# Nyström attention and sticky experts on one core: the preload of w1 behind batch 1's first sums, with other filling products, transfers and score halves in the start-up

## The chip, the core and the metric

The kernel runs on one core of one Trainium2 chip. The metric is the device time of one execution in microseconds; 451.7 us is the median of 3 runs of the kernel before (451.6 to 452.22). The engines are named as in the profile: PE (TensorE matmul), PEld (its weight loads), DVE (VectorE), ACT (ScalarE), POOL (GpSimd), SP (SyncE, which issues nearly all transfers).

## What is computed

For each of 8 batches a Nyström attention with 8 heads, 576 tokens and 32 landmarks is computed, and its output goes through one of 8 experts per token; the expert of a token may stick to that of the token before it.

```python
def sm(a, b):
    s = scale * np.matmul(a, b.transpose(0, 1, 3, 2)); s = s - np.max(s, axis=-1, keepdims=True)
    e = np.exp(s); return e / (np.sum(e, axis=-1, keepdims=True) + 1e-09)
A, Bm, C = sm(q, k_lm), sm(q_lm, k_lm), sm(q_lm, k)      # q_lm, k_lm: means over 18 tokens, 32 of them
Z = Bm.T / (norm1(Bm) * norminf(Bm) + 1e-06)
for _ in range(6):
    Z = 2 * Z - Z @ Bm @ Z
x = A @ Z @ C @ v                                        # (8 batches, 576 tokens, 512)
logits = x @ w_gate; local = sigmoid(x @ w_local)
# per token: e = argmax(logits) if local < 0.5 or first token, else the expert of the token before
out = softmax(logits)[e] * (relu(x @ w1[e]) @ w2[e])     # w1[e]: 512 x 1024, w2[e]: 1024 x 512
```

## The kernel before

Work is done batch by batch. For each batch one "own" expert, the one that most of its tokens chose, is applied to all 576 tokens; tokens of other experts are gathered later into extra slots. x is never formed: w1 is first multiplied by the small matrix `wt` (`w_w1`, L1247, 16 matmul records; PSUM result split into a high part `gh` on ACT and a low part `gl` on DVE, `split_g`), and then `mm1` (L1295) multiplies that with the attention weights `at` (high and low part, `ath` and `atl`). Per block f of 128 hidden units `mm1` has six products, in the order gh ath, gh atl, gl ath for each half g of the heads; their relu goes through ACT and DVE, and the products with w2 follow (L1337). The eight blocks f are made in two passes over the tokens.

The order on each engine is written out by hand: every engine runs its instructions in program order, `at_time` hangs steps into a clock that `expert` advances, and `startup` is a plain list. `startup` does batch 0's attention and parts of batch 1's. Its order around the change:

- Before anything else PE multiplies zeros with zeros (L190: 11 products of 512 columns, L192: 18 of 16 columns), into a tile that nobody reads. PE's next step is `score_c(0, 0)` (L965).
- SP issues all loads of batches 0 and 1, and then (L945) `firsts`: of every one of the 8 experts the first 128 hidden units of w1, 2 MB, so that they are there when the expert becomes known. After that SP issues nothing until the write of `wt` (L751) and that of the attention weights (L1165).
- POOL computes half sums of batch 1's landmarks (`lk0_half`, L310) between two steps of batch 0's softmax (`sa_max`, L1070).
- When the vote on the gates has written the expert's number into `regs` (L875), PE fills the time with 3 `keep_busy` products and 22 narrow ones (L1175); SP and PE load the number into a register; SP issues the expert's w1 and w2 (`load_w1`, L1232, f = 1, 2, 3 and two pairs, and `get_w2`, L1274); PE multiplies the preloaded piece (`first_w1`, L1257), which gives block f = 0.
- `second_block` (at clock 0.02) begins with batch 1's scores of landmarks against all keys (`c_products`, L621): 512 columns and then 96, each for 4 places c and 2 halves g of the heads, each product on a 64 x 32 part of the array. Between them stand the w1 products of block f = 1; behind them on DVE the maximum over the first bank (`c_max`, L631) and then the low parts `gl` (L1269) of block 1. The w1 products of blocks 2 and 3 follow at clock 1.005, the scores' other steps from 1.3 on, batch 0's `fresh` (L845 to L855) at 1.6, the second half of w1 at 2.8.

PE's float32 products are recorded as two matmul records each.

Of the kernel before, what the change touches and what calls it, by code (L numbers as in the profile page):

```python
# [24 lines left out]
P = 128  # L25
# [38 lines left out]
def nystrom_attn_then_sticky_moe(ctx, tc, qT, kT, v, wg, w12, out):  # L64
    nc = tc.nc
# [122 lines left out]
    pz = one.tile([P, 512])  # L188
    for _ in range(11):
        nc.tensor.matmul(pz, zeros[:, 0:P], zeros, start=True, stop=True)  # L190
    for _ in range(18):
        nc.tensor.matmul(pz[:, 0:16], zeros[:, 0:P], zeros[:, 0:16], start=True, stop=True)  # L192
# [419 lines left out]

    def c_products(st, k0, n):


        out, x = (st["pc"][1], 0) if k0 == 512 else (st["pc"][0], k0)
        for c in range(4):
            for g in range(2):
# [314 lines left out]
    def startup(st, nx):  # L933
# [10 lines left out]
        firsts = pre.tile([P, E, 512], F32, name="w1f")  # L944
        nc.sync.dma_start(out=firsts, in_=w12[:, 0, :, 0:512].rearrange("e p x -> p e x"))  # L945
        sc = sm.tile([P, 2, 3], F32, name="sc0", bufs=1)
# [147 lines left out]
        lk0_half(0)  # L1094
        lk0_half(1)
        score_a(1, 1, (py, "py"))
        newton_add(1)
# [73 lines left out]
        vote(st, lq0)  # L1171
        keep_busy(3)
        pz = one.tile([P, 512])
        for _ in range(22):
            nc.tensor.matmul(pz[:, 0:16], ones, ones[:, 0:16], start=True, stop=True)  # L1175

        e = st["e"] = expert_of(regs[0:1, 0:1], (ET.SP, ET.PE))
        st["w1", 0] = load_w1(e, 0, ((nc.sync, 1, 1, 0, P), (nc.sync, 2, 1, 0, P), (nc.sync, 3, 1, 0, P)))
        get_w2(0, 0)
        get_w2(0, 1)  # L1180
        st["w1", 1] = load_w1(e, 1, ((nc.sync, 0, 2, 0, P), (nc.sync, 2, 2, 0, P)))
        get_w2(0, 2)
# [14 lines left out]
        def second_block():  # L1197
            c_begin(nx, (one, one))
            c_begin_rest(nx, (one, Banks((pg, "pg"))))
            c_products(nx, 0, 512)  # L1200
            lk2(0)
            lk2(1)
            g1 = w_w1(st, 0, 1, 1, ((py, "py"), (py, "py")))
            next(g1)
            c_products(nx, 512, 96)
            c_max(nx, 1, (0,))
            at_once(g1)

        at_time(0.02, second_block)
        at_time(0.6, c_max, nx, 1, (1,))  # L1210
        at_time(1.005, lambda: at_once(w_w1(st, 0, 2, 2, ((py, "py"), (py, "py")))))
        at_time(1.3, c_max, nx, 0)
        at_time(1.31, c_exp_b, nx)
# [626 lines left out]
```

## Time and profile before

| | kernel before |
|---|---|
| median of 3 runs | 451.7 us (451.6 to 452.22) |
| the profiled execution: its time | 451.21 us |
| the profiled execution: its span | 449.4 us |
| PE, PEld, DVE, ACT, POOL busy | 435.1, 337.1, 284.5, 216.0, 192.0 us |
| granted TensorE clock | 1.00 of full in every slice |
| HBM read and written | 75.27 and 15.47 MB |

The span runs from the first to the last instruction; the execution's time has some 2 us around it. PE is busy nearly throughout; what it does in the first 45 us is partly filling. Rows below are of this one profiled execution. In a row of the time line, the first two numbers are the start and the length in us, and a bracket at the end holds the idle time of the engine before it and what ended it. A line number is that of a helper where one records the work.

### The profile page before, as it was taken

The numbers are of one execution on the slowest core, as the hardware profiler recorded it, in microseconds if no ns is written. First come the engines' busy times: TensorE is split into PE (matmuls) and PEld (weight loads), VectorE is DVE, ScalarE is ACT, GpSimd is POOL, SyncE is SP. The second block draws the span as 40 slices with busy tenths as digits, with TensorE's granted clock in tenths as the row PEclk, the third lists the DMA queues.
The fourth block names the chain that finished last, engine by engine and source line by source line (L and its number), as shares of the span: only waits on it lengthen the run. The fifth ranks groups of instructions, "written<-read, shape, count | busy, mean of one in ns | idle before, by whom it ended". The sixth has DMA issues, their size and how long they took to land.

```text
span 449.4 us, 12512 instructions
## 1 busy us (share of the span) xinstructions
PE 435.1 (97%) x4898; PEld 337.1 (75%) x4898; DVE 284.5 (63%) x869; ACT 216.0 (48%) x577; POOL 192.0 (43%) x235
## 2 busy tenths in 40 slices
PE   8888999999999999999999999999999999999996
PEld 3455777777786788878887788788887778776885
DVE  7878786666858576665766574656555786954111
ACT  2546525467354751566253752465145414445611
POOL 5456663165815664263632650174116601055520
PEclk9999999999999999999999999999999999999999
DMA  8959952779569697649957615831164315692211
GB/s 303 378 198 350 367 190 98 268 287 261 210 160 382 202 388 159 245 164 341 290 138 260 237 54 125 318 110 48 55 233 158 113 44 173 252 313 95 97 31 50
DMA packets 62365, 91.53 MB, mean 204 GB/s; under 512 B 26731, under 2 KB 28267, under 8 KB 61152
## 3 DMA queue, kind: packets, MB, share of 16 engines
q1 hardware_dynamic: 60960, 86.23, 57.0%
q0 software_dynamic: 1344, 4.48, 2.7%
q8 instruction: 39, 0.64, 0.6%
q14 instruction: 22, 0.18, 0.1%
HBM read 75.27 MB, written 15.47 MB: 202 GB/s over the span
## 4 chain that ended last, share of the span: by engine, by line
PE 77%; DVE 13%; ACT 5%; issue 2%; DMA 1%; POOL 1%; SPq 0%; DVEq 0%; ACTq 0%; POOLq 0%
PE py L1337 33%; PE ph L1295 19%; PE pg L1346 5%; PE ph L1247 2%; PE one L416 2%; PE one L463 1%; DVE h L1307 1%; PE one L562 1%; PE py L1573 1%; DMA k_t<-kT 1%; PE one L517 1%; DVE gl L1269 1%; PE one L825 1%; POOL t L265 1%; DVE sk L261 1%
## 5 line engine op out<-in xcount | busy, mean ns | idle before, releaser
L1337 PE MATMUL py<-wh,h 128*128 128x512 f32 x504 | 161.6, 403 | 0.1
L1284 POOL TENSOR_TENSOR wl<-raw,wh 128x512 fp32r<-128x512 f32 x64 | 82.2, 1293 | 70.8 <-ACT wh L1282 69.7
L1302 ACT ACTIVATE h<-ph 128x256 fp32r<-128x256 f32 (+1 forms) x128 | 52.4, 413 | 111.2 <-PE ph L1295 94.2
L1337 PEld LDWEIGHTS py<-wh,h 128*128 128x128 f32 x504 | 86.4, 189 | 25.2 <-issue 13.2
L1307 DVE SCALAR_TENSOR_TENSOR h<-ph,h 128x256 fp32r<-128x256 f32 x128 | 53.0, 416 | 61.0 <-ACT h L1302 58.2
L1337 PE MATMUL py<-wl,h 128*128 128x512 f32 x252 | 80.5, 400 | 0.0
L1295 PE MATMUL ph<-ath,gh 128*128 128x320 f32 (+1 forms) x256 | 77.5, 303 | 1.5 <-ACT gh L1266 0.8
L1295 PE MATMUL ph<-ath,gl 128*128 128x320 f32 (+1 forms) x256 | 75.8, 296 | 0.0
L1295 PE MATMUL ph<-atl,gh 128*128 128x320 f32 (+1 forms) x256 | 75.6, 295 | 0.0
L1295 PEld LDWEIGHTS ph<-ath,gh 128*128 128x128 f32 x256 | 48.4, 189 | 9.1 <-ACT h L1302 2.2
L1337 PEld LDWEIGHTS py<-wl,h 128*128 128x128 f32 x252 | 45.9, 188 | 11.6 <-issue 1.3
L1295 PEld LDWEIGHTS ph<-atl,gh 128*128 128x128 f32 x256 | 48.3, 189 | 3.9
L1295 PEld LDWEIGHTS ph<-ath,gl 128*128 128x128 f32 x256 | 48.3, 189 | 0.2 <-DVE gl L1269 0.2
L1282 ACT CAST wh<-raw 128x512 fp32r<-128x512 f32 x69 | 43.2, 627 | 2.2 <-DMA raw<-w 1.4
L1406 POOL TENSOR_TENSOR ys<-ys,yl 64x512 f32<-64x512 f32 x8 | 10.3, 1281 | 58.5 <-ACT yl L1404 58.5
L265 POOL TENSOR_TENSOR t<-q_t 128x288 f32<-128x288 f32 x20 | 14.5, 747 | 23.5 <-DVE sk L267 23.5
L423 DVE TENSOR_TENSOR et<-et,one 128x64 f32<-128x64 f32 x36 | 7.9, 220 | 24.7 <-ACT et L422 16.4
L794 POOL TENSOR_TENSOR sa<-sa,rsa 128x1152 f32<-128x1152 f32 x7 | 14.9, 2133 | 19.9 <-DVE s L693 13.2
L265 POOL TENSOR_TENSOR t<-k_t 128x288 f32<-128x288 f32 x22 | 17.0, 795 | 11.9 <-DVE sq L267 10.8
L1346 PE MATMUL pg<-wl,h 128*128 128x512 f32 x56 | 21.9, 391 | 0.0
L1346 PE MATMUL pg<-wh,h 128*128 128x512 f32 x56 | 21.8, 390 | 0.0
L1395 ACT ACTIVATE ys<-py,token 128x512 f32<-128x512 f32 x30 | 19.0, 685 | 5.0 <-PE py L1337 4.7
(435 smaller groups left out, 729.3 us busy)
## 6 DMA issues: line engine op xcount, KB each, us to landing
raw<-w SPq DMA_DIRECT2D x75, 256.0 KB
raw<-w SPq DMA_DIRECT2D x16, 1024.0 KB
k_t<-kT SPq DMA_DIRECT2D x9, 1152.0 KB
q_t<-qT SPq DMA_DIRECT2D x9, 1152.0 KB
out<-ys SPq DMA_DIRECT2D x31, 256.0 KB
v_t<-v SPq DMA_DIRECT2D x20, 256.0 KB
ad<-sa POOLq DMA_DIRECT2D x7, 576.0 KB, 3.1
v_t<-v SPq DMA_DIRECT2D x3, 1024.0 KB
```

What stands on the lines that cost most here:

```text
L265: nc.gpsimd.tensor_add(t9[:, i], src[:, a + i, :, 0:9], src[:, a + i, :, 9:18])
L416: return {1: lambda: each_place(lambda g, r: nc.tensor.matmul(pn[r, g, :], et[r, g, 0:32], et[r, g, n0:64], start=True, stop=True))}, part ...
L794: nc.gpsimd.tensor_tensor(out=sa, in0=sa, in1=rs.unsqueeze(2).broadcast_to([P, 2 * NJ, M]), op=ALU.mult)
L1282: by(out=wh, in_=raw)
L1284: rest.tensor_tensor(out=wl, in0=raw, in1=wh.bitcast(F32), op=ALU.subtract)
L1295: mm = nc.tensor.matmul(hp, w[:, g, c], x[:, g, s0:s0 + n], start=(i == 0), stop=(i == 5))
L1302: nc.scalar.activation(out=h[:, 0:e], in_=hp[:, 0:e], func=AF.Relu)
L1307: nc.vector.scalar_tensor_tensor(out=h[:, 384:384 + m], in0=hp[:, 0:m], scalar=0.0, in1=h[:, 0:m].bitcast(F32), op0=ALU.max, op1=ALU.subtract)
L1337: nc.tensor.matmul(yps[k], h[:, part + i * P:part + i * P + P], w, start=(f == 0 and part == 0 and w is wh), stop=(f == NC2 - 1 and part = ...
L1346: nc.tensor.matmul(yps[4], hs[ff][1], w, start=(ff == 0 and w is w2[ff][0]), stop=(ff == NC2 - 1 and w is w2[ff][1]))
L1395: nc.scalar.mul(out=ys, in_=yp, mul=st["pw"][:, k:k + 1])
L1406: nc.gpsimd.tensor_tensor(out=ys[0:64], in0=ys[0:64], in1=yl[0:64], op=ALU.add)
```

## The change

The head has 12 wide and 34 narrow products. `firsts` is issued after a one-element memset by POOL that stands behind POOL's two `lk0_half` sums, so that SP waits for these before it issues the load. After the vote, 5 `keep_busy` products stand in place of 3 and 22 narrow ones. w1's first half is loaded as block 1 and the pair 2, 3, its second half in one transfer. `c_products` takes the places c it is to do: the 512-column scores are done for places 0 and 1 ahead of block 1's w1 products and for places 2 and 3 behind them, and the 96-column scores move behind the w1 products of blocks 2 and 3.

```diff
     pz = one.tile([P, 512])
-    for _ in range(11):
+    for _ in range(12):
         nc.tensor.matmul(pz, zeros[:, 0:P], zeros, start=True, stop=True)
-    for _ in range(18):
+    for _ in range(34):
         nc.tensor.matmul(pz[:, 0:16], zeros[:, 0:P], zeros[:, 0:16], start=True, stop=True)
...
-    def c_products(st, k0, n):
+    def c_products(st, k0, n, places=range(4)):
...
-        for c in range(4):
+        for c in places:
             for g in range(2):
...
         firsts = pre.tile([P, E, 512], F32, name="w1f")
-        nc.sync.dma_start(out=firsts, in_=w12[:, 0, :, 0:512].rearrange("e p x -> p e x"))
...
         lk0_half(0)
         lk0_half(1)
+        nc.gpsimd.memset(firsts[0:1, 0, 0:1], 0.0)
+        nc.sync.dma_start(out=firsts, in_=w12[:, 0, :, 0:512].rearrange("e p x -> p e x"))
         score_a(1, 1, (py, "py"))
...
         vote(st, lq0)
-        keep_busy(3)
-        pz = one.tile([P, 512])
-        for _ in range(22):
-            nc.tensor.matmul(pz[:, 0:16], ones, ones[:, 0:16], start=True, stop=True)
+        keep_busy(5)
 
         e = st["e"] = expert_of(regs[0:1, 0:1], (ET.SP, ET.PE))
-        st["w1", 0] = load_w1(e, 0, ((nc.sync, 1, 1, 0, P), (nc.sync, 2, 1, 0, P), (nc.sync, 3, 1, 0, P)))
+        st["w1", 0] = load_w1(e, 0, ((nc.sync, 1, 1, 0, P), (nc.sync, 2, 2, 0, P)))
         get_w2(0, 0)
         get_w2(0, 1)
-        st["w1", 1] = load_w1(e, 1, ((nc.sync, 0, 2, 0, P), (nc.sync, 2, 2, 0, P)))
+        st["w1", 1] = load_w1(e, 1)
...
             c_begin_rest(nx, (one, Banks((pg, "pg"))))
-            c_products(nx, 0, 512)
+            c_products(nx, 0, 512, (0, 1))
             lk2(0)
             lk2(1)
             g1 = w_w1(st, 0, 1, 1, ((py, "py"), (py, "py")))
             next(g1)
-            c_products(nx, 512, 96)
+            c_products(nx, 0, 512, (2, 3))
             c_max(nx, 1, (0,))
             at_once(g1)
...
         at_time(1.005, lambda: at_once(w_w1(st, 0, 2, 2, ((py, "py"), (py, "py")))))
+        at_time(1.007, c_products, nx, 512, 96)
         at_time(1.3, c_max, nx, 0)
```

## Rows read from the trace of the kernel before

**Rows 1.** The page: each engine's busy us, share of the span and instructions.

```profile
PE 435.1 (97%) x4898; PEld 337.1 (75%) x4898; DVE 284.5 (63%) x869; ACT 216.0 (48%) x577; POOL 192.0 (43%) x235
```

**Rows 2.** Chain of waits, 0 to 80 us: start, length, engine, tile and line.

```profile
7.33 0.37 DVE nm L977
...
25.51 0.46 issue
```

**Rows 3.** Time line, 0 to 22 us: the head of PE, DVE's landmark sums.

```profile
1.23 4.88 PE L190 MATMUL one<-sa 128*128 128x512 bf16 x11 [1.23 <-DVE sa L180]
...
5.90 0.65 PE L192 MATMUL one<-sa 128*128 128x16 bf16 x18
...
6.49 0.69 PE L965 MATMUL one<-k_t,ql 64*32 64x288 f32 x8
...
7.62 1.40 DVE L261 TENSOR_REDUCE sq<-q_t 128x32 f32<-128x576 f32 x2
...
8.99 1.50 DVE L261 TENSOR_REDUCE sk<-k_t 128x32 f32<-128x576 f32 x2
```

**Rows 4.** Time line around the expert's choice: PE and ACT.

```profile
27.73 0.81 PE L930 MATMUL one<-ones 128*128 128x512 bf16 x3
28.38 0.70 PE L1175 MATMUL one<-ones 128*128 128x16 bf16 x22
29.31 1.13 PE L1257 MATMUL py<-w1f,ys 128*128 x8 [0.24 <-ACT ql L275]
...
29.75 0.26 ACT L275 ACTIVATE ql<-sq 128x64 f32<-128x64 f32 x1 [0.46 <-DVE sq L313]
30.03 0.27 ACT L1266 CAST gh<-py 128x128 fp32r<-128x128 f32 x1
```

**Rows 5.** Time line: POOL's half sums, SP's issues of the first w1 pieces.

```profile
18.42 1.45 POOL L310 TENSOR_TENSOR h<-k_t 128x288 f32<-128x288 f32 x2
...
29.00 1.43 SPq L1232 DMA_DIRECT2D raw<-w  x3
```

**Rows 6.** Stretches: length, busy by engine, granted clock, DMA share, GB/s.

```profile
20.00:23.00 3.00, 2.49 (x77) 1.23 (x65) 2.52 (x10) 1.40 (x5) 2.85 (x3) 1.00 1.04 386
...
27.20:29.90 2.70, 2.46 (x38) 1.76 (x37) 2.41 (x9) 0.41 (x2) 1.56 (x3) 1.00 0.00 0
30.00:32.40 2.40, 2.40 (x27) 1.37 (x27) 1.30 (x4) 1.17 (x6) 1.29 (x2) 1.00 0.83 288
```

**Rows 7.** Time line of the second block, PE, PEld and DVE.

```profile
31.46 1.09 PE L621 MATMUL one<-k_t,ql 64*32 64x512 f32 x16
...
32.39 0.18 PEld L1247 LDWEIGHTS py<-raw,wt 64*32 64x32 f32 x16 [0.75 <-DMA raw<-w]
...
32.64 0.69 DVE L631 TENSOR_REDUCE nm8c<-one 128x1 f32<-128x512 f32 x1 [0.86 <-PE one L621]
...
33.25 0.48 DVE L1269 TENSOR_TENSOR gl<-py,gh 128x128 fp32r<-128x128 f32 x2
...
33.27 0.41 PE L1295 MATMUL ph<-ath,gh 128*128 128x320 f32 x1 [0.25 <-ACT gh L1266]
...
33.67 0.34 PE L1295 MATMUL ph<-ath,gl 128*128 128x320 f32 x1
...
35.56 0.41 PE L1295 MATMUL ph<-ath,gh 128*128 128x320 f32 x1 [0.53 <-ACT gh L1266]
```

**Rows 8.** Time line: scores of all places and both halves of the heads.

```profile
42.66 0.71 PE L771 MATMUL one<-q_t,k_t 64*32 64x288 f32 x16
```

**Rows 9.** Time line, 37 to 40 us: POOL, DVE and PE.

```profile
37.58 1.29 POOL L1284 TENSOR_TENSOR wl<-raw,wh 128x512 fp32r<-128x512 f32 x1
37.59 1.34 DVE L849 SCALAR_TENSOR_TENSOR eq<-pe,keys 128x40 f32<-128x40 f32 x1
...
39.94 0.59 PE L1247 MATMUL ph<-raw,wt 64*32 64x512 f32 x1 [0.97 <-DVE atl L1310]
```

**Rows 10.** The same line of DVE from 36 us on: ns min/median/max, first and last start.

```profile
L849 DVE SCALAR_TENSOR_TENSOR eq<-pe,keys x8: 199/201/1344, 37.6 to 367.3; 128x40 f32<-128x40 f32 x8
```

## The prediction

> **What bounds the kernel now.** I read the page's busy shares first: PE is busy for 97% of the span [rows 1], so from the moment the expert products run without gaps, any delay of PE's work is carried to the end, and any idle time that is saved comes off it. All six hunks of the change lie in the first 45 us, so the question is how much later or earlier that steady part begins. The chain of waits for this stretch [rows 2] shows who sets it: from about 7 us to the choice of batch 0's expert it runs mostly over DVE, one step releasing the next, and one piece of 0.46 us at 25.51 is "issue", a halt of PE that no wait explains. Then I read the time line of the head [rows 3], of the stretch around the expert's choice [rows 4], of the transfers [rows 5 and 6] and of the block in which batch 0's first hidden products and batch 1's key scores alternate [rows 7].
>
> The profiled execution took 451.21 us, 0.5 us under the median of the three runs, 451.7. I make the sum as a difference in the profiled execution and add it to the median.
>
> **The head of PE: 12 wide and 34 narrow products instead of 11 and 18.** The eleven wide products take 4.88 us [rows 3], so they start about 0.43 us apart: 512 columns in 0.43 us is the 1.2 GHz level (the granted clock is shown as 1.00 here). At 27.73 three of the same width take 0.81 us in all [rows 4], about 0.21 us apart, the 2.4 GHz level. The narrow ones stand 0.03 us apart: 18 in 0.65 us, of which the last one's own length is about 0.17. After them batch 0's first key scores start at 6.49, though the query landmarks they need were ready earlier; PE's order holds them. The added work is 16 x 0.025 to 0.028 = 0.40 to 0.45 us, plus one wide product, 0.21 us if the clock has already risen and 0.43 us if not: 0.61 to 0.88 us. The first matrix products with real data run at the fast level, so the rise falls near the end of the wide ones; I take 0.70. It ends up on the path: the maximum over these scores starts on DVE at about 7.3, right behind a landmark sum [rows 2], and the scores' end (6.49 + 0.69 = 7.18) left it about 0.05 us to spare. The later landmark sums of DVE queue behind that maximum. They give back about 0.1: the two key sums take 1.50 us against 1.40 for the two query sums [rows 3], since they were waiting a little for their data. So DVE is 0.70 - 0.05 - 0.1 = about 0.55 us later, and the chain up to the expert's choice has no other slack that I can see. **+0.55**, bounds +0.4 and +0.75.
>
> **The preload behind batch 1's first sums.** The one-element memset stands on POOL behind the two half sums that end at 18.42 + 1.45 = 19.87 [rows 5], in the changed kernel 0.55 later, so SP issues the preload near 20.5. Behind it on SP stand only two writes to DRAM that start some 4 us later, so nothing is held up by SP's wait. From issue to first bytes takes about 1 us: the first w1 piece is issued at 29.00 [rows 5], nothing moves up to 29.9, and then 288 GB/s do [rows 6]. The 2.1 MB of the preload at 386 GB/s [rows 6] are 5.4 us, so they end near 27. That first w1 piece (0.26 MB) ends a wait of PE's weight loads at 32.39 [rows 7], so it lands about then: 1 us to start, 0.7 us of transfer, and so up to 1.7 us until the last queue is done. With that tail the preload is there by 28.7. The products that read it start at 29.31 [rows 4], then 29.8: at least 1.1 us of cover. The two writes to DRAM (0.7 MB, 1.9 us) move behind the preload and end near 29, before the expert's own w1 can flow (30.5). Before, these engines were idle from 27.2 to 29.9 [rows 6], and that is the space it takes. Nothing on the chain waits for a transfer between 17 and 29 us, so the move itself gains nothing: **0**. Its memset, about 0.1 us on POOL, is covered by DVE's other work. If the cover fails, each microsecond of lateness is a microsecond of the kernel.
>
> **Tail of the start.** 22 narrow products go, two wide ones come (0.43 us, at the 0.21 apart above). PE sits idle for 0.24 us before the first w1 products [rows 4], which wait for the expert's number in a register, so at most 0.24 is to be had. But the copy behind them on ACT starts at 30.03, right at the end of another ACT operation (29.75 + 0.26) [rows 4], which doesn't move. **0**, bounds -0.2 and 0.
>
> **w1 in fewer transfers.** SP saves one issue of about 0.5 us (three take 1.43 [rows 5]) ahead of w2 and a second one ahead of w2's third block. The piece that PE waits for (f = 1) stays first in the queue; the pair f = 2, 3 was long there when its products ran. **0**, bounds -0.3 and 0.
>
> **The large scores in halves.** Half the score products don't take half the time. Products on different corners of the array run side by side: 8 matmul records of 288 columns take 0.69 us [rows 3], 16 take 0.71 us [rows 8]. So each half of the 512-column scores takes about as long as the whole did, 1.09 us [rows 7]. The first half hides where the whole did, in the wait for w1 that ends at 32.39. The second half starts when the w1 products have streamed through, about 32.65, and ends near 33.7. Two things wait for it. PE: the hidden products of f = 1 began at 33.27, now near 33.5. DVE, worse: the maximum over the scores started at 32.64, just when they were ready, and now starts near 33.7; behind it in DVE's order stand the two low parts of g, started at 33.25, now near 34.3. PE's third hidden product, at 33.67, needs the first of these, and gets it near 34.6: **+0.97** at this point. The 96-column scores that moved out need about 0.4 us and fall into the 0.53 us in which PE waits for ACT at 35.56 [rows 7]: 0. If that cover were gone they would cost 0.4.
>
> How much of 0.97 is left at 40 us? There PE stood still for 0.97 us until 39.94, on DVE [rows 9]. DVE was late because a 40-element operation took 1.34 us; its seven other instances take about 0.2 [rows 10]. It began at 37.59, together with a POOL operation of 1.29 us [rows 9], and ended with it. With everything before it 0.97 later, DVE reaches this group inside POOL's operation rather than ahead of it, waits only for the rest of it, and still has two short operations (0.2 us each) to do after it where before it had the end of one: PE can go on about 0.3 us later than before (0.2 and a step between engines), not 0.97. **+0.3**, bounds 0 and +0.97.
>
> On this stall the Trainium skill, "SBUF — State Buffer", "Who interferes with whom", says that a VectorE operation with two SBUF inputs is fully blocked by a GpSimd operation that reads SBUF, until that one finishes. By it the remainder of POOL's operation is what counts, 452.5 in all; if the 1.14 us were instead a property of this one operation, they would move with it, 453.2 in all. The row, 1344 ns against 201, agrees with the rule.
>
> **Sum.** 0.55 + 0 + 0 + 0 + 0.3 = +0.8 us (rounded down): 452.0 for an execution like the profiled one, **452.5** beside the median.
>
> **The rivals.**
> - *Slower, the stall passes through.* The 0.97 us of the halves isn't taken up at 40 us, because POOL's operation, which starts when its w2 block has landed, moves as well, or because w1's second half, now one transfer, lands late. Then 0.55 + 0.97 = 1.5: 453.2, up to 453.7 with the head's upper bound and the moved scores. It decides from the point where PE reaches the second half of w1 after DVE does. For it: the margins at 40 us are some tenths. Against it: rows 9 and 10.
> - *Slower, the preload is late.* It lands after the first w1 products could start. It decides when its transfer takes over 1.1 us longer than I reckon, and each further one counts fully; with 1 us over, 453.5. Against it: two idle microseconds [rows 6].
> - *Absorbed.* DVE's delay at the head is taken up, or the halves cost nothing because PE was going to wait anyway: between 451.7 and 452.2. This is also the case in which the change does not do what it says, as where a transfer sets the pace.
> - *Faster, the halt or the clock.* The halt at 25.51 sits between products that wait for nothing; DVE's input for the ones after them was ready at once, so some 0.4 us are lost. If it comes from PE's instructions being late under the preload's traffic, then another place of the preload and another count of instructions ahead of it can remove it. And if the clock rises later in most executions than in this one (the median is 0.5 over it), a longer head may bring it up before the scores: 16 records of 0.69 us would take some 0.5 us more at the slow level. Together with the transfers' 0.3 and the tail's 0.2, against the rest of the sum, some 450.7. Against it: this trace shows no late rise, and the preload still flows at 25 us.
>
> Of the halt, the Trainium skill ("Runtime: NRT & Kernel Launch", "Instruction fetch mechanics") says that instructions are fetched ahead in blocks and that crossing a block is mostly hidden. By it the halt isn't the preload's, and the faster rival loses 0.4; the row of 0.46 us of "issue" speaks against "hidden" in this one place, and no row names the cause.
>
> **How the numbers follow.** The forecast, 452.5 with a range of its own of 451.9 to 453.1: 0.38. Stall passes through, 453.2: 0.24. Late preload, 453.5: 0.04. Absorbed, 452.0: 0.18. Faster, 450.7: 0.16. A measurement tells about 0.2% from no change, 0.9 us: below 450.8 is faster, above 452.6 slower. Faster 0.12 (the faster rival but for a quarter). Slower 0.41: 0.16 of the forecast, which stands close to the bound, 0.21 of the first rival and 0.04 of the late preload. Same 0.47. The range leaves out the far half of the faster rival and the top of the slower ones: 451.0 to 453.6.
>
> **What would show it.** Right: the first scores on PE near 7.2 instead of 6.49 and all of DVE's later start-up work half a microsecond later; the preload issued near 20.5 with its products not waiting; DVE's maximum over batch 1's scores a microsecond later relative to the w1 products, and a new idle of some 0.7 us on PE in the hidden products of f = 1; the 40-element operation short. Wrong: the head's products end before the landmarks are ready, the halt at 25.5 is gone, or the second half of w1 on PE starts no later than 39.94, or over 1.2 us later.

## The result and the profile after

The changed kernel takes 455.18 us in the median of 5 runs (454.09 to 456.72), the kernel before 451.70 (451.06 to 452.54). The ratio is 1.0076 with a 95% interval of 1.0050 to 1.0103: slower by 3.4 us (2.3 to 4.7). The prediction, 452.5 with a range of 451.0 to 453.6, was wrong: the kernel is 1.6 us above its upper end.

| | before | after |
|---|---|---|
| the profiled execution: its time | 451.21 us | 456.72 us |
| the profiled execution: its span | 449.4 us | 454.9 us |

The page of the changed kernel, busy time by engine, against [rows 1]:

```profile
PE 436.6 (96%) x4895; PEld 337.1 (74%) x4895; DVE 285.1 (63%) x869; ACT 215.8 (47%) x577; POOL 192.0 (42%) x236
```

The work is the same within 1.5 us on every engine. The span grew by 5.5 us: what was added is waiting. The following table follows single steps of the program through both traces. Only the last column matters: between two rows where it rises, time was lost.

| step (line before) | before | after | later by |
|---|---|---|---|
| batch 0's first key scores on PE (L965) | 6.49 | 7.28 | 0.79 |
| products of wt with the gate weights (L757) | 24.26 | 24.90 | 0.64 |
| the expert's number on DVE (L874) | 27.92 | 28.01 | 0.09 |
| first w1 products (L1257) | 29.31 | 31.48 | 2.17 |
| w1 products of f = 1 (L1247) | 32.39 | 34.57 | 2.18 |
| third hidden product of f = 1 (L1295) | 33.67 | 36.88 | 3.21 |
| w1's second half (L1247) | 39.94 | 43.62 | 3.68 |
| scores of all places (L771) | 42.66 | 46.34 | 3.68 |

From there to 150 us the shift on PE stays within 3.67 to 3.74 us, as rigid as the prediction took the steady part to be. The profiled execution is the slowest of the five and loses 1.8 us more behind 150 us; half of that, 0.89 us, is one more halt of PE at 161.85 us that no wait explains (its kind is told with e8). The medians differ by 3.5, which is what the first 46 us show, so these are what has to be explained.

The time line of the changed kernel from 20 to 32 us (start, length, engine, line; in the bracket the idle time before and what ended it), against [rows 4, 5]:

```profile
20.43 0.09 POOL L1095 MEMSET w1f<- 1x1 f32 x1
20.55 0.39 SPq L1096 DMA_DIRECT2D w1f<-w  x1
...
25.68 0.99 PE L825 MATMUL pg<-at,wgc 128*32 128x160 f32 x16
...
28.01 0.17 DVE L874 TENSOR_REDUCE best<-one 128x1 int32<-128x8 f32 x1
...
29.93 1.42 POOL L310 TENSOR_TENSOR h<-k_t 128x288 f32<-128x288 f32 x2
...
31.48 1.13 PE L1256 MATMUL py<-w1f,ys 128*128 x8 [2.42 <-POOL h L310]
```

Two things stand here that the kernel before doesn't have. The gates' products (L825) run through without the halt of 0.46 us of [rows 2], and so the number is known only 0.09 us later although everything before it is 0.63 later. And PE then stands still for 2.42 us ahead of the first w1 products, where it stood for 0.24 [rows 4]. The profile puts that wait down to POOL's half sums, which end at 31.35. This is one of the cases in which a wait for several semaphores has to be looked at twice: in the records of single instructions PE's wait for the preload's semaphore ends at 31.375, and the last of the preload's 16 parts landed at 31.35, too. The experiments tell the two apart.

The stretches of the changed kernel (length, busy time by engine, granted clock, DMA share, GB/s), against [rows 6]:

```profile
20.00:22.00 2.00, 1.49 (x88) 1.18 (x80) 1.93 (x8) 0.30 (x1) 2.00 (x4) 1.00 0.18 39
22.00:24.00 2.00, 1.79 (x34) 0.59 (x22) 1.59 (x6) 1.42 (x5) 1.53 (x2) 1.00 0.97 248
24.00:26.00 2.00, 1.75 (x29) 0.75 (x29) 2.00 (x6) 1.49 (x5) 1.83 (x3) 1.00 1.04 226
26.00:28.00 2.00, 1.93 (x28) 1.03 (x24) 1.61 (x6) 1.15 (x4) 1.40 (x2) 1.00 0.97 300
28.00:30.00 2.00, 1.06 (x5) 0.29 (x3) 1.76 (x6) 0.42 (x2) 1.57 (x3) 1.00 1.05 383
```

The engines of the DMA are busy (0.97 to 1.05), but the preload moves at 226 to 300 GB/s for six microseconds and not at the 386 of [rows 6]. It takes 9.6 us from issue until 15 of its 16 parts are there (30.19), and 10.8 until the last is.

The time line of the changed kernel from 36 to 44 us, against [rows 7, 9]:

```profile
36.73 0.61 POOL L1281 CAST wh<-raw 128x512 fp32r<-128x512 f32 x1 [5.37 <-DMA raw<-w]
36.88 0.42 PE L1294 MATMUL ph<-ath,gl 128*128 128x320 f32 x1 [0.51 <-DVE gl L1268]
...
40.59 0.61 POOL L1281 CAST wh<-raw 128x512 fp32r<-128x512 f32 x1
40.64 0.61 DVE L847 TENSOR_TENSOR pe<-lg,mxl 128x40 f32<-128x40 f32 x1
...
41.28 1.28 POOL L1283 TENSOR_TENSOR wl<-raw,wh 128x512 fp32r<-128x512 f32 x1
41.29 1.33 DVE L849 SCALAR_TENSOR_TENSOR eq<-pe,keys 128x40 f32<-128x40 f32 x1
...
43.30 0.21 DVE L1309 SCALAR_TENSOR_TENSOR atl<-ph,atl 128x64 fp32r<-128x64 f32 x1
...
43.62 0.59 PE L1246 MATMUL ph<-raw,wt 64*32 64x512 f32 x1 [1.35 <-issue]
```

The third hidden product waits for the low part of g as forecast (0.51 us). But POOL's first w2 block is there only at 36.73, so that its three blocks run one after the other until 42.56, and DVE's short operations of 40 elements (L847, L849) meet the two operations of the third block: each ends within 0.1 us of POOL's operation. The wait of PE ahead of w1's second half has become 1.35 us instead of 0.97 [rows 9].

### The profile page after: what moved, and what is told of

Its sections match the earlier page's. It is cut to its first block, busy times and chain, and to the rows that moved or that the text cites. A ratio compares the mean times of both kernels' runs of the same rounds, so it can differ in the third digit from the quotient of the medians.

```text
span 454.9 us, 12504 instructions
## 1 busy us (share of the span) xinstructions
PE 436.6 (96%) x4895; PEld 337.1 (74%) x4895; DVE 285.1 (63%) x869; ACT 215.8 (47%) x577; POOL 192.0 (42%) x236
## 4 chain that ended last, share of the span: by engine, by line
PE 74%; DVE 13%; ACT 6%; POOL 3%; issue 2%; DVEq 0%; ACTq 0%; POOLq 0%
PE py L1336 32%; PE ph L1294 19%; PE pg L1345 5%; PE ph L1246 2%; PE one L416 2%; PE one L463 1%; PE one L562 1%; DVE h L1306 1%; PE py L1572 1%; PE one L190 1%; DVE gl L1268 1%; PE one L517 1%; PE one L825 1%; POOL t L265 1%; ACT ys L1394 1%
## 5 line engine op out<-in xcount | busy, mean ns | idle before, releaser
L1306 DVE SCALAR_TENSOR_TENSOR h<-ph,h 128x256 fp32r<-128x256 f32 x128 | 53.0, 416 | 60.9 <-ACT h L1301 56.5
L265 POOL TENSOR_TENSOR t<-k_t 128x288 f32<-128x288 f32 x22 | 17.0, 795 | 10.8 <-DVE sq L267 10.8
```

Source lines behind the costliest of these rows:

```text
L265: nc.gpsimd.tensor_add(t9[:, i], src[:, a + i, :, 0:9], src[:, a + i, :, 9:18])
L1306: nc.vector.scalar_tensor_tensor(out=h[:, 384:384 + m], in0=hp[:, 0:m], scalar=0.0, in1=h[:, 0:m].bitcast(F32), op0=ALU.max, op1=ALU.subtract)
```

## The experiments

The theory after the two traces: of the 3.7 us, 2.1 are the preload's transfer, which is late; the halves cost about 1 us; and the halt that vanished hides the head's cost. The rivals: PE waits for POOL through the memset and not for the transfer; the halt has to do with the head's count of instructions and not with the preload; the halves alone make the wait at 43 us. Runs are compared with runs of the kernel before on the same chip, in turn with them; from one such series to another its median went from 450.3 to 451.7 us, so a ratio says more than a time. Steps are read from one execution of each kernel.

### One part undone, and one part alone

**e1_preload_first: the changed kernel, the preload where it was.**

```diff
         firsts = pre.tile([P, E, 512], F32, name="w1f")
+        nc.sync.dma_start(out=firsts, in_=w12[:, 0, :, 0:512].rearrange("e p x -> p e x"))
...
-        nc.gpsimd.memset(firsts[0:1, 0, 0:1], 0.0)
-        nc.sync.dma_start(out=firsts, in_=w12[:, 0, :, 0:512].rearrange("e p x -> p e x"))
```

> The changed kernel with the preload issued where it was before the change, ahead of everything (no memset); all other parts of the change stay. Theory A, the preload is late: the first w1 products start near 29.4 to 29.7 us instead of 31.48, and w1's second half on PE, at 43.62 in the changed kernel and 39.94 before, starts near 41.4, because the score halves alone still cost 1.1 us at the hidden products of f = 1 and 0.4 behind them; median about 453.1. Rival B, the preload costs all and the halves nothing: second half near 40, median 451.7 to 452.0. Rival C, the preload's place costs nothing and something else holds the first w1 products: 31.4 and 455.

Measured: ratio 1.0021 (1.0006 to 1.0036), about 0.95 us; first w1 products at 29.66, w1's second half at 40.53:

```profile
29.66 1.13 PE L1255 MATMUL py<-w1f,ys 128*128 x8 [0.15 <-issue]
...
40.53 0.59 PE L1245 MATMUL ph<-raw,wt 64*32 64x512 f32 x1
```

Theory A was right on the first, and too high on the second by 0.9: without the late preload the halves are nearly taken up at 40 us. So the rest of the change costs 0.95, where the prediction's sum was 0.8, and the preload's place the other 2.5.

**e2_hold_only: the kernel before with the held-back preload.**

```diff
-        nc.sync.dma_start(out=firsts, in_=w12[:, 0, :, 0:512].rearrange("e p x -> p e x"))
...
         lk0_half(0)
         lk0_half(1)
+        nc.gpsimd.memset(firsts[0:1, 0, 0:1], 0.0)
+        nc.sync.dma_start(out=firsts, in_=w12[:, 0, :, 0:512].rearrange("e p x -> p e x"))
```

> The kernel before with the held-back preload alone (memset on POOL and the transfer behind it). Theory A: the transfer is issued near 19.9 and needs 8 to 11 us, so the first w1 products start between 29.8 and 31.0 instead of 29.31, and everything later moves by as much: median 452.2 to 453.4. If the late end is that of one queue of the sixteen which also carries an instruction fetch, fifteen queues are done 1 us or more before it. Rival C: products at 29.31, median 451.7.

Measured: ratio 1.0042 (1.0023 to 1.0061), 1.9 us. The number is known at 27.32 (0.6 sooner than before: no halt), and the profile of this one names the wait. Its time line:

```profile
27.32 0.17 DVE L874 TENSOR_REDUCE best<-one 128x1 int32<-128x8 f32 x1
...
29.73 1.13 PE L1258 MATMUL py<-w1f,ys 128*128 x8 [1.25 <-DMA w1f<-w]
```

The transfer was issued at 19.86 and 15 of its 16 parts were there at 29.47, the last at 29.59. Theory A's range for the first w1 products, 29.8 to 31.0, was missed by 0.1 below, and its range for the median, 452.2 to 453.4, by 0.2 above (453.61). These products start 0.4 us later than in the kernel before, but w1's second half 1.6, so most of the loss comes behind them:

```profile
37.09 0.61 POOL L1283 CAST wh<-raw 128x512 fp32r<-128x512 f32 x1 [6.40 <-DMA raw<-w]
...
41.56 0.59 PE L1248 MATMUL ph<-raw,wt 64*32 64x512 f32 x1 [1.46 <-DVE atl L1311]
```

As in the changed kernel, POOL gets its first w2 block late and PE waits ahead of w1's second half, which comes 11.84 us behind the first w1 products (before: 10.63). There are no halves here: the late preload costs this 1.2 us without them.

**e3_head_only: the kernel before with the head.**

```diff
-    for _ in range(11):
+    for _ in range(12):
...
-    for _ in range(18):
+    for _ in range(34):
```

> The kernel before with the head alone (12 wide, 34 narrow). Theory A: the start-up chain runs 0.63 us later up to the gates' products at 25 us, and there PE's halt of 0.46 us is gone, because its instructions stand at other places; the expert's number is known 0.1 us later than before; median 451.8. The prediction's reading: the halt stays or has nothing to do with the head, the number is known 0.55 to 0.65 us later; median 452.3.

Measured: ratio 1.0015 (1.0003 to 1.0028), 0.7 us; the scores start at 7.19 and the number is known at 28.45, 0.53 later. The prediction had 0.55. Theory A fell here: the halt stays, so the head doesn't remove it. But it stands elsewhere. The chain of waits (start, length, what) of this kernel:

```profile
24.81 0.24 PE ph L757 x7
25.05 0.35 issue
25.41 0.26 PE ph L757 x9
```

With 17 more products at the head the halt comes between the 7th and the 8th record of L757; before it came behind the fifth record of L825 (25.04 to 25.51), 16 matmul records later in PE's program. e1 has it at the same place as e3 (0.63 us), e4 where the kernel before has it (0.27). So its place goes by the count of PE's instructions.

**e4_halves_only: the kernel before with the scores in halves.**

```diff
-            c_products(nx, 0, 512)
+            c_products(nx, 0, 512, (0, 1))
...
-            c_products(nx, 512, 96)
+            c_products(nx, 0, 512, (2, 3))
...
+        at_time(1.007, c_products, nx, 512, 96)
```

> The kernel before with the scores in halves alone, and the 96-column scores moved. Theory A: the third hidden product of f = 1 starts 1.0 us later, and nothing is given back at 40 us, because PE's wait there moves with POOL's operation and its stalled neighbour on DVE: w1's second half at 41.0 to 41.4 instead of 39.94, median 452.8 to 453.2. The prediction's reading: 1.0 us at the stall, of which 0.3 is left at 40 us: 40.2 there, median 452.0.

Measured: ratio 1.0007 (0.9993 to 1.0020), 0.3 us; no difference is shown. Its time line:

```profile
32.47 1.04 PE L621 MATMUL one<-k_t,ql 64*32 64x512 f32 x8
...
33.57 0.69 DVE L631 TENSOR_REDUCE nm8c<-one 128x1 f32<-128x512 f32 x1 [2.01 <-PE one L621]
...
34.18 0.48 DVE L1270 TENSOR_TENSOR gl<-py,gh 128x128 fp32r<-128x128 f32 x2
...
34.51 0.41 PE L1296 MATMUL ph<-ath,gl 128*128 128x320 f32 x1 [0.51 <-DVE gl L1270]
...
38.27 0.72 DVE L847 TENSOR_TENSOR pe<-lg,mxl 128x40 f32<-128x40 f32 x1
...
39.03 0.20 DVE L849 SCALAR_TENSOR_TENSOR eq<-pe,keys 128x40 f32<-128x40 f32 x1
...
40.23 0.59 PE L1248 MATMUL ph<-raw,wt 64*32 64x512 f32 x1 [0.33 <-issue]
```

The first w1 products start at 29.08 here. Counted from them, the third hidden product comes after 5.43 us (before: 33.67 - 29.31 = 4.36), 1.07 later, and w1's second half after 11.15 (before: 10.63), 0.52 later. L849 takes 0.20 us and not 1.34, and L847 ahead of it 0.72 where before it took 0.21 (37.34): DVE meets only the rest of POOL's operation. This is the prediction's reading, with 0.5 left where it had 0.3.

**e5_tail_transfers: the kernel before with the tail and the fewer w1 transfers.**

```diff
-        keep_busy(3)
-        pz = one.tile([P, 512])
-        for _ in range(22):
-            nc.tensor.matmul(pz[:, 0:16], ones, ones[:, 0:16], start=True, stop=True)
+        keep_busy(5)
...
-        st["w1", 0] = load_w1(e, 0, ((nc.sync, 1, 1, 0, P), (nc.sync, 2, 1, 0, P), (nc.sync, 3, 1, 0, P)))
+        st["w1", 0] = load_w1(e, 0, ((nc.sync, 1, 1, 0, P), (nc.sync, 2, 2, 0, P)))
...
-        st["w1", 1] = load_w1(e, 1, ((nc.sync, 0, 2, 0, P), (nc.sync, 2, 2, 0, P)))
+        st["w1", 1] = load_w1(e, 1)
```

> The kernel before with the tail (5 wide products for 3 wide and 22 narrow) and the fewer w1 transfers alone. The prediction's reading: both cost and bring nothing at the start of w1's second half (39.94 before): 39.7 to 40.1, ratio 0.999 to 1.001. Rival: w1's second half, now one transfer, lands after PE needs it, or its third block is later: 40.3 or more, ratio above 1.002.

Measured: ratio 1.0002 (0.9990 to 1.0014): nothing, as forecast. Counted from the first w1 products (28.57), w1's second half comes after 10.54 us (before: 10.63). In this execution PE doesn't halt near 25 us, although the preload is first: the halt varies from execution to execution, and with it all that follows, by some 0.6 us.

The parts alone nearly add up to the whole. The ratios of e3, e4 and e5 lie 0.0024 over 1 together, and that of e1, which has these three, 0.0021; with e2 it is 0.0066, and 0.0076 for the whole change.

### What the first w1 products wait for

**e7_hold_sooner: the changed kernel, memset and preload ahead of the half sums.**

```diff
         sa_max(0)
+        nc.gpsimd.memset(firsts[0:1, 0, 0:1], 0.0)
+        nc.sync.dma_start(out=firsts, in_=w12[:, 0, :, 0:512].rearrange("e p x -> p e x"))
         lk0_half(0)
         lk0_half(1)
-        nc.gpsimd.memset(firsts[0:1, 0, 0:1], 0.0)
-        nc.sync.dma_start(out=firsts, in_=w12[:, 0, :, 0:512].rearrange("e p x -> p e x"))
```

> The changed kernel with the memset and the preload behind batch 0's first softmax step on POOL, so ahead of batch 1's two half sums: issued about 1.4 us earlier, near 19.1. Theory A, the transfer's end is what the first w1 products wait for: they start between 29.4 and 30.1 us instead of 31.48, and POOL's first w2 block, at 36.7 in the changed kernel, comes 1.4 us or more earlier; median 452.5 to 453.7. Rival B, the products wait for POOL (the memset makes them depend on it) and not for the transfer: they stay at 31.4 and the median at 455.

**e9_half_preload: the changed kernel with half of the preload's bytes.** It leaves out the pieces of experts 4 to 7; batch 0's expert is among the others.

```diff
-        nc.sync.dma_start(out=firsts, in_=w12[:, 0, :, 0:512].rearrange("e p x -> p e x"))
+        nc.sync.dma_start(out=firsts[:, 0:4], in_=w12[0:4, 0, :, 0:512].rearrange("e p x -> p e x"))
```

> The changed kernel with half of the preload's bytes: only experts 0 to 3 are loaded ahead (1 MB instead of 2.1), the others are left out, and batch 0's expert is among those loaded. Theory A, bytes and queue set the time: the preload ends near 26 us, the first w1 products start at 29.2 to 29.5, and of the 3.7 us at 46 us some 1.5 are left; median 452.7 to 453.3. Rival B, the products wait for POOL: 31.4 and 455.

**e12_split_in_after: the changed kernel, only half of the preload held back.**

```diff
         firsts = pre.tile([P, E, 512], F32, name="w1f")
+        nc.sync.dma_start(out=firsts[:, 0:4], in_=w12[0:4, 0, :, 0:512].rearrange("e p x -> p e x"))
...
-        nc.gpsimd.memset(firsts[0:1, 0, 0:1], 0.0)
-        nc.sync.dma_start(out=firsts, in_=w12[:, 0, :, 0:512].rearrange("e p x -> p e x"))
+        nc.gpsimd.memset(firsts[0:1, 4, 0:1], 0.0)
+        nc.sync.dma_start(out=firsts[:, 4:E], in_=w12[4:E, 0, :, 0:512].rearrange("e p x -> p e x"))
```

> The changed kernel with only the second half of the preload (experts 4 to 7) held back, the first half issued where the kernel before issues it. Theory A: as with half of the bytes, the held part ends near 26.5, the first w1 products start at 29.0 to 29.4 instead of 31.48, w1's second half at 39.9 to 40.3 instead of 43.62; ratio to before 1.000 to 1.004. Rival: the place of the memset on POOL or the dependence on it is what costs; 31.4, ratio 1.007.

Measured: e7 1.0050 (1.0026 to 1.0075), e9 1.0036 (1.0015 to 1.0057), e12 1.0022 (1.0008 to 1.0036). In all three the first w1 products start as soon as the register is loaded: at 29.05, 29.08 and 29.20, in e7 and e9 some tenths sooner than theory A had it. The chain of waits of e12:

```profile
29.20 0.91 PE py L1257 x6
```

The time line of e9, in which the order on every engine is that of the changed kernel:

```profile
20.32 0.38 SPq L1096 DMA_DIRECT2D w1f<-w  x1
...
29.08 1.13 PE L1256 MATMUL py<-w1f,ys 128*128 x8 [0.24 <-issue]
29.72 1.45 POOL L310 TENSOR_TENSOR h<-k_t 128x288 f32<-128x288 f32 x2
```

PE runs these products ahead of the half sums to which the profile of the changed kernel attributes the wait. So it was the transfer, and the name in the bracket was that of a neighbour that happened to end at the same time. w1's second half starts at 40.02, 39.92 and 39.96 in the three, against 43.62: with the preload in time the later part of the loss is gone as well. e12 keeps all bytes and everything else of the change, and its ratio equals that of e1, so the lateness of the second half of the bytes is what the hold-back costs. The totals of e7 and e9 go down less than the steps, 2.2 and 1.6 us over the kernel before. Of e7 this stays unexplained: its profiled execution is the fastest of five (450.71, the others up to 454.13), and where the others lose is in no trace.

The table has the moments of the transfer in the kernels that hold all of it back, and in e9, from the records of its 16 parts and of the 16 KB instruction packets that the same DMA engines carry:

| | issue | 15 parts | last part | 16 KB packet near the end | first w1 products |
|---|---|---|---|---|---|
| after | 20.55 | 30.19 | 31.35 | 28.79 to 29.82 | 31.48, waited |
| e10 | 20.48 | 30.16 | 31.20 | 28.32 to 29.34 | 31.34, waited |
| e14 | 20.16 | 29.62 | 30.86 | 27.98 to 29.00 | 31.00, waited |
| e2 | 19.86 | 29.47 | 29.59 | 29.08 to 30.11 | 29.73, waited |
| e7 | 18.61 | 28.49 | 28.66 | 28.02 to 29.03 | 29.05 |
| e8 | 18.47 | 28.37 | 28.96 | 24.68 to 25.72 | 30.51 |
| e9, half the bytes | 20.32 | 26.48 | 26.56 | 26.09 to 27.11 | 29.08 |

From issue to the 15th part it is 9.5 to 9.9 us for 2.1 MB in all six, and 6.2 for half of it. The last part comes 1.0 to 1.2 us behind in three kernels; there an instruction packet of 1.0 us runs within the transfer's last two microseconds. Where the packet comes just as the transfer ends (e2, e7, e9), the last part is 0.1 to 0.2 behind; in e8, where it ran three microseconds before the end, 0.6. The transfer that SP issues next (L751) agrees: in e2 and e9, with the packet just ahead of its end, its last part comes 1.18 and 1.44 us behind its 15th, where the preload's was 0.1 behind. That the packet holds up one part is what these rows suggest; no run moved the packet alone, so it isn't shown.

**e8_before_hold_sooner: the kernel before with the held-back preload, placed as in e7.**

```diff
         sa_max(0)
+        nc.gpsimd.memset(firsts[0:1, 0, 0:1], 0.0)
+        nc.sync.dma_start(out=firsts, in_=w12[:, 0, :, 0:512].rearrange("e p x -> p e x"))
         lk0_half(0)
```

> The kernel before with the held-back preload alone, placed as in e7: issued near 18.5. Theory A: PE's halt near 25 us stays away, as it did with the later place, so the expert's number is known 0.4 to 0.6 us sooner than before; the preload is there between 28.0 and 28.8, so that the first w1 products start at 28.7 to 29.0 instead of 29.31 and the kernel gains up to 0.6: median 451.1 to 451.7. Rival B: the earlier transfer makes PE's instructions late again, the halt is back and nothing is gained: 451.7 to 452.3. Rival D: the pieces of w1 and w2 behind it still come late, and over 0.5 us is lost at 40 us: 452.2 to 453.

Measured: ratio 1.0077 (1.0047 to 1.0107), 3.5 us. Rival B was right, and by more than it said: the number is known 1.2 us later than before, and the scores of all places come 1.3 later (43.99). In the profiled execution most of the rest is a second halt, 1.55 us at 159.41; whether the other three executions have it isn't known. The chain of waits of e8:

```profile
25.07 0.40 PE pg L825 x3
25.47 1.70 issue
27.17 0.52 PE pg L825 x10
```

The halt is at the place of the kernel before, and 1.70 us long. Its 16 KB packet ran from 24.68 to 25.72. PE's program is the same in e2; there the packet ran from 20.14 to 21.72, and there is no halt. With the preload first the packet starts at 22.6 to 23.2, against 19.8 to 20.3 in the five kernels that issue the held-back load near 20 (after, e2, e9, e10, e14), none of which halts. Where PE halts it goes on 1.4 to 1.7 us behind the packet's end: 25.97 behind 24.60 before, 25.41 behind 23.75 in e1, 25.40 behind 23.98 in e3, 25.74 behind 24.14 in e4, 27.17 behind 25.72 in e8; e7, whose packet comes between the two groups, halts for 0.20 us until 24.80, behind 23.40. In e5 the packet ends at 23.90, just soon enough.

Counted from PE's first product, the halt near 25 us stands behind 346 matmul records (before, e4, e8) or 347 (e1, e3, e7), whether 17 of them were added at the head or not. Two later halts without a wait stand at such fixed counts, too: behind 2117 or 2118 records, at 157 to 162 us, for 0.86 to 1.55 us (the changed kernel, e1, e5, e8, e9, e13), and behind 2750 or 2751, at 207 to 209 us, for 0.25 to 0.91 us (e3, e4, e7, e11, e12). The one of the changed kernel, in its chain of waits:

```profile
161.85 0.89 issue
```

All 17 of these halts end 1.3 to 1.7 us behind the end of a 16 KB packet. The places lie 1,771 and 633 records apart, 14.1 and 5.0 times the 126 matmul records that come on average to one of the 39 such packets of an execution. So the halt is PE waiting for its instructions: where, the count of instructions decides; how long, when the packet comes. Near 25 us it is data on the DMA engines that push the packet back. At 160 us the packet starts at 156.2 to 160.5 in the six kernels that halt and at 150.3 to 153.9 in the ten others; what pushes it there isn't known. (That the 16 KB packets are PE's is read from this agreement; the records don't name an engine.) One execution of each kernel was traced, so whether an edit makes the later halts likelier isn't shown; a single execution's total can be off by as much.

On this the Trainium skill, "Runtime: NRT & Kernel Launch", "Instruction fetch mechanics", says that instructions are refilled in blocks of 16 KiB over a DMA queue and that crossing a block is mostly hidden. The packets agree with the size; "mostly hidden" doesn't hold behind a long transfer, where the runs show 0.20 to 1.70 us.

### The wait ahead of w1's second half

**e10_fresh_later and e14_fresh_26: the changed kernel with fresh at clock 2.1, and at 2.6.**

```diff
-        at_time(1.6, fresh, st)
+        at_time(2.1, fresh, st)
```

> The changed kernel with the step fresh (the short operations of 40 elements on DVE) hung at clock 2.1 instead of 1.6. Theory A: at 41 to 43 us these operations wait for POOL's w2 blocks and hold up the relu step that PE's second half of w1 waits for; without them ahead of it PE's wait of 1.35 us shrinks to under 0.3, so w1's second half starts at 42.3 to 42.6 instead of 43.62; median 453.9 to 454.3. Rival: PE waits there for w1's second half itself or for ACT; 43.5 and 455.

```diff
-        at_time(1.6, fresh, st)
+        at_time(2.6, fresh, st)
```

> The changed kernel with the step fresh at clock 2.6, which puts its five short operations on DVE behind the two relu steps that PE's second half of w1 waits for (at 2.1 they still stood ahead of them). Theory A: in the changed kernel the short operations wait for POOL's w2 blocks and delay these relu steps; with them out of the way PE's wait of 1.35 us ahead of w1's second half falls under 0.3 us, and this part starts 10.9 to 11.3 us behind the first w1 products instead of 12.1; ratio to before 1.004 to 1.007. Rival: PE waits there for w1's second half (its last queue lands at 39.9) or for its instructions: 12.0 behind, ratio 1.007 or more.

Measured: e10 1.0090 (1.0058 to 1.0122), e14 1.0068 (1.0049 to 1.0087). At 2.1 the order on DVE is still that of the changed kernel, so e10 tells nothing of fresh and stands as a second execution of it (first w1 products at 31.34, a wait of 1.3 us ahead of w1's second half). At 2.6 the short operations stand behind the relu steps, and the time line of e14 is this:

```profile
40.57 1.29 POOL L1283 TENSOR_TENSOR wl<-raw,wh 128x512 fp32r<-128x512 f32 x1
40.70 0.42 DVE L1306 SCALAR_TENSOR_TENSOR h<-ph,h 128x256 fp32r<-128x256 f32 x1 [0.74 <-ACT atl L1303]
41.04 0.21 DVE L1309 SCALAR_TENSOR_TENSOR atl<-ph,atl 128x64 fp32r<-128x64 f32 x1
41.43 0.61 PE L1246 MATMUL ph<-raw,wt 64*32 64x512 f32 x1
...
42.15 0.19 DVE L847 TENSOR_TENSOR pe<-lg,mxl 128x40 f32<-128x40 f32 x1
42.38 0.20 DVE L849 SCALAR_TENSOR_TENSOR eq<-pe,keys 128x40 f32<-128x40 f32 x1
```

PE's wait is gone: w1's second half comes 10.43 us behind the first w1 products, and not 12.14 as in the changed kernel or 11.44 as in e10, whose f = 1 products came sooner. From the third hidden product of f = 1 it is 5.30 us against 6.73 and 6.71. The relu step (L1306) runs at its usual 0.42 us beside POOL's operation, and the short operations, now after it, take 0.2 each. So it was they that held up PE, and they were slow because of POOL. The total changed less than this wait (the intervals of 1.0076, 1.0090 and 1.0068 overlap), so how much of it is kept to the end isn't shown.

The Trainium skill, "SBUF — State Buffer", "Who interferes with whom", says that a VectorE operation with two SBUF inputs and a GpSimd operation that reads SBUF exclude each other, while one with at most one SBUF input, outside VectorE's two-port modes, doesn't contend with GpSimd. The trace agrees: L847 and L849 read two tiles in SBUF and end with POOL's operation, L1306 reads PSUM and one tile and doesn't wait.

### A kernel that might beat both

**e11_split_preload: the kernel before, half of the preload first and half held back.** The diff is that of e12, made on the kernel before.

> The kernel before with half of the preload (experts 0 to 3) issued where it was and the other half behind batch 1's half sums, after a memset as in the change. Theory A: a fetch of PE's instructions waits behind data already queued on its DMA engine; with nothing queued beyond 21 us it is served by then instead of at 23.2, PE's halt at 25.5 (0.46 us) goes, and the second half, 1 MB, lands 6.2 us after its issue, near 26, well ahead of need. So the first w1 products start at 28.6 to 28.9 instead of 29.31: ratio 0.9980 to 0.9995. Rival: the second half's own traffic brings the halt back, or the late half holds the products: 29.2 or later, ratio 1.000 to 1.004.

**e13_split_tail_transfers: e11 and e5 together.**

> The kernel before with the preload in two halves as in e11, and the tail and the fewer w1 transfers as in e5. Theory A: PE's halt near 25 us is gone as in e11 and the first w1 products wait for the expert's number alone, so they start at 28.5 to 28.8 and w1's second half at 39.1 to 39.6; ratio 0.9975 to 0.9995, at or below that of e11 (0.9991). Rival: the two do not add, or e11's gain was the scatter of executions: ratio 0.9995 to 1.001.

**e15_split_fresh: e11 with fresh at clock 2.6.**

> The kernel before with the preload in two halves as in e11, and fresh at clock 2.6. Theory A: PE's wait of 0.97 us at 39.94 in the kernel before is the same one, so it falls under 0.3 as well: w1's second half starts 10.0 to 10.2 us behind the first w1 products instead of 10.63, near 38.8 to 39.1; ratio 0.9970 to 0.9990. Rival: what is gained there is lost where fresh stands now, or in the scatter of executions: ratio 0.999 to 1.001.

Measured: e11 0.9991 (0.9981 to 1.0001), e13 0.9997 (0.9985 to 1.0009), e15 1.0000 (0.9982 to 1.0018). In all three the halt is gone (16 KB packet at 20.5 to 21.2, number known at 27.25 to 27.48) and the first w1 products start at 28.75 to 28.88, half a microsecond sooner than before. None is shown to be faster: the gain that e11 may have, 0.4 us, is at the edge of its interval, and e13 and e15 came out as their rivals said. In e13 it is lost again at 40 us, where the short operations met POOL once more (a wait of 1.25 us, w1's second half at 39.98). In e15 that part starts at 39.05, now waiting 0.65 us for its own transfer, and the total still equals that of the kernel before.

## Why the prediction was wrong

**The preload's move, 0 in the sum: this step failed.** It had 8.2 us from issue to the last part (20.5 to 28.7) and 1.1 us of cover. The transfer took 9.6 us until the 15th part and 10.8 until the last, 2.6 more, and the products were ready for it sooner, at 29.4 (28.01 and the 1.39 us which before lie between the number and these products, 29.31 - 27.92), because the halt was gone; the prediction had 29.8. So 31.48 - 29.40 = 2.1 us passed: 1.5 by the transfer (2.6 less the cover), 0.4 by the sooner need, and the rest from the last part to the products. Of the transfer's 2.6 us, 1.9 come from a wrong row: 386 GB/s was the rate of the preload behind other loads. The row of a transfer that starts on idle engines stood beside it, 288 GB/s in 30.0 to 32.4 [rows 6]. By that row 2.1 MB take 7.3 us, with 1 us of start and 1.7 of tail 10.0, and the end would have come at 30.5, 0.7 us behind the need as the prediction had it. Reading the right row would have put a late preload into the sum, and not among the rivals with a chance of 0.04. The rest, from 30.5 to the last part at 31.35, stands in no row of the kernel before. Two of the prediction's own signs of being wrong came with it: the halt is gone, and w1's second half is 3.7 us late.

**The halves, 0.97 at the stall and 0.3 left.** By itself this step held: 1.07 and 0.5 in e4. In the changed kernel it didn't, through the preload: w2's blocks queued behind it, POOL began them at 36.73, and DVE's short operations met them after all. Between the first w1 products and w1's second half the changed kernel lost 1.5 us (12.14 against 10.63) where e1, e7, e9 and e12, with the same halves, lost 0.1 to 0.3; e10, the same order once more, lost 0.8, and e2, with the late preload and no halves, 1.2. From the third hidden product of f = 1 to w1's second half it is 6.3 us before, 5.3 to 5.7 with the halves and a preload in time (e1, e4, e7, e9, e12), and 6.7 to 6.8 with a late one (the changed kernel, e10, e2). So what fails at 40 us is not the reading of the halves: the late preload takes the slack, 1.0 to 1.4 us of it, that was to give most of their 0.97 back. The rival "the stall passes through" named this mechanism, "POOL's operation, which starts when its w2 block has landed, moves as well"; it was not joined with the late preload, which makes it happen.

**The head, +0.55.** Right in size: 0.53 in e3, an execution like that which the sum was made for. But the size belongs to the execution. The products of wt with the gate weights (L757) start at 24.36 to 24.90 us in the eight traced kernels with this head and at 24.14 to 24.37 in the eight without, 0.44 later in the mean. The head's own length differs: its wide products stand 0.43 us apart at first and 0.22 later, in e9 from 4 us on, in the kernel before up to the last of them at 0.43. So e9's scores start at 6.23, sooner than before, and yet its L757 products at 24.68: there something else than the head holds DVE's chain. In the changed kernel the vanished halt hides the head. The faster rival had that mechanism, PE's instructions late under the preload's traffic, and put 0.4 us on it; e1, e2 and e8 show it.

**Tail and transfers, 0.** Right, 0.0002 in e5. The fear that w1's second half lands late in one transfer didn't come true: PE's wait at 43 us went away without it (e14).

Added up by the steps of the two traces: 0.1 (head less halt) + 2.1 (preload) + 1.0 (halves at the stall) + 0.5 (behind it, mostly the short operations beside POOL; with the preload in time 0.6 to 1.0 came back here) = 3.7 us at 46 us, and 3.4 to 3.5 in the medians.

## What to carry to other kernels

A load that is moved to a later point has to be priced as it will run there: from idle engines, to its last part, with whatever else these engines carry, and by the trace's row of a transfer that starts like that. What stands behind it in the queue is late as well, and that can undo a slack elsewhere (here DVE's short operations beside POOL) that the sum had counted on. A long transfer issued early isn't free either: an engine's instructions come over the same DMA engines, so a halt that nothing explains is to be laid beside the instruction packets, and its place counted in records of its engine.

## What the runs showed of the hardware

- A 2.1 MB load issued to idle or nearly idle DMA engines took 9.5 to 9.9 us until 15 of 16 parts had landed (six kernels); in the changed kernel its first packet started 1.06 us behind the issue, and of its 1024 packets of 2 KB half took 84 ns or less, but 182 over 150 ns, the longest 549 (mean 119; 213 from 25 to 26 us). Where the same load ran behind others 2 packets took over 150 ns (mean 89). Why isn't shown.
- PE's halts without a wait, 17 of 0.20 to 1.70 us in 16 traces, end 1.3 to 1.7 us behind a 16 KB instruction packet and stand behind 346 or 347, 2117 or 2118, 2750 or 2751 matmul records, so that 17 products put ahead of the place shift what is interrupted, not the count.
- The load of the expert's number into PE's register took 490 ns before and 759 in the changed kernel, where the DMA engines moved 383 GB/s at that time instead of 1 or less; in e2, e10 and e14, whose preload ran past it, too, it took 533, 569 and 762, in all others 484 to 492.
- PE's products of zeros, begun at 1.23 us, ran at the 1.2 GHz level (wide products 0.43 us apart) up to 4.0 us in e9 and to the last wide one, 5.9 us, in the kernel before; in e9 those behind it stand 0.22 apart, the 2.4 GHz level.
